# Maxout, output and w1·w_out products of a pooled-attention kernel: pairs of float16 scaled by powers of two in place of pairs of float32r

## The chip, the cores and the metric

The kernel runs on one core of one Trainium2 chip. Its time is the device time of one launch, in microseconds, as the median of three runs. The engines in the profile are PE (TensorE: matmuls, with PEld for the loads of stationary operands), DVE (VectorE), ACT (ScalarE), POOL (GpSimd) and SP (SyncE, which issues the DMAs). "hi" and "lo" below are the two halves of a number that is split so that two short numbers together carry its digits.

## The reference

```python
# attention: B=4, N=384*32=12288 queries, C=128, kv pooled 4x4 -> 768 keys a batch
kv_pool = kv.reshape(B, H // r, r, W // r, r, C).mean(axis=(2, 4))
k = v = kv_pool.reshape(B, -1, C) @ w_sr
s = (q @ k.transpose(0, 2, 1)) / sqrt(C)
a = exp(s - s.max(-1)); a /= a.sum(-1) + 1e-9
x = (a @ v).reshape(B * N, C)                       # 49152 x 128
# maxout: w1, w2, w3 are 128 x 768, w_out is 768 x 128
h = maximum(maximum(x @ w1, x @ w2), x @ w3)
out = h @ w_out
```

The four maxout weights arrive as float64; the kernel reads their 64-bit words as integers and builds float32 from them itself.

## The kernel before

**Tiles.** The 49152 queries go through in 96 groups of 512 (`NG`), 24 to a batch. A group is turned so that channels lie on the partitions. For each group there are four score tiles of 128 queries by 768 keys (six matmuls of 384 columns each, into `ps_s`), a softmax, the product with the values (`attend`, 18 matmuls of 512 columns into `ps_x`), and the maxout part in six slices `f` of 128 hidden units.

**Maxout.** With d2 = w2 − w1 and d3 = w3 − w1 the hidden value is x·w1 + max(0, x·d2, x·d3). So `hidden` (L610) makes two products a slice, x·d2 and x·d3, `hidden_first` (L621, ACT) and `hidden_max` (L626, DVE) take max(0, ·, ·), `hidden_hi` (L631, ACT) and `hidden_lo` (L636, POOL) split the result, and `project` (L691) multiplies by w_out. The part x·w1·w_out comes from one 128×128 matrix `w1o`, made once by `product_w1` (L259), and is added after the last slice.

**Pairs.** Scores and values already use pairs of float16. The maxout products use pairs of float32r: x as `xh`, `xl` (L594, L602), the d's as `d_hi`, `d_lo`, h as `hh`, `hl`, w_out as `wo`, and `w1o`. Every product is three matmuls: hi·hi, hi·lo, lo·hi. That gives 36 + 18 + 3 = 57 float32r matmuls of 512 columns a group.

**Order.** Nothing is reordered by a scheduler: every engine runs its instructions in the order of the program (`InOrder`, L94). The table `ORDER` (L151) writes out, for twelve slices (two groups), which step is issued when: H hidden, R relu, M max, C hi, L lo, O project, S scores, m/e/c/l softmax, X attend, xh/xl the split of x, P/G/T the output, q. the queries, k the keys of the next batch. `WEIGHTS` (L149) is such a table for the start: for each of the four weights and both halves, at which point n the steps of taking the 64-bit words apart are issued (power_bits, power_float, sign, join, rest). The points 0 to 22 lie in the written-out start (L792 to L879), the later ones in the first slices through `late` (L881).

**Buffers.** `ps_h` has two banks, one for each of the two products of a slice, so the next slice's first product needs the relu of this one, and its second needs the max. `spare(True)` (L112) borrows one of these banks for small matmuls. `ps_s` has two double banks, `ps_x` and `ps_o` one bank each.

**Keys.** For each batch a class `Keys` pools kv, finds one power of two from the largest pooled value (`size`, `sized`), and splits the projected keys. For batches 1 to 3 its steps are spread over the groups r of the batch before by `keys_step` (L1004).

Of the kernel before, what the change touches and what calls it, by code (L numbers as in the profile page):

```python
# [9 lines left out]
F32 = mybir.dt.float32  # L10
F32R = mybir.dt.float32r
# [10 lines left out]
def kernel(  # L22
# [28 lines left out]

    nc = tc.nc
# [20 lines left out]
    X_UP, O_DOWN = 2.0 ** -24, 2.0 ** -10  # L73
# [41 lines left out]
    def pow2(t, src):  # L115

        dve.tensor_scalar(
            out=t.bitcast(I32), in0=src.bitcast(I32), scalar1=EXPO, scalar2=None, op0=ALU.bitwise_and
        )
        dve.tensor_scalar(out=t, in0=t, scalar1=TINY, scalar2=HUGE, op0=ALU.max, op1=ALU.min)  # L120
# [11 lines left out]
    x_up = const.tile([C, 1], F32, name="x_up")  # L132
    d_hi = [[const.tile([C, HALF_F], F32R, name=f"d{i}{h}_hi") for h in range(2)] for i in (2, 3)]
    d_lo = [[const.tile([C, HALF_F], F32R, name=f"d{i}{h}_lo") for h in range(2)] for i in (2, 3)]
    w1T = [const.tile([P, HALF_F], F32, name=f"w1T{h}") for h in range(2)]
    w1o = const.tile([C, 2, C], F32R, name="w1o")
    e_bias = const.tile([P, 1], F32, name="e_bias")
    wo = [const.tile([P, NFT // 2, 2, C], F32R, name=f"wo{h}") for h in range(2)]
# [5 lines left out]
    JOIN_ON_POOL, REST_ON_DVE, LO_ON_DVE, HI_ON_DVE, HL_ON_DVE, W_HI_ON_DVE = ((0, 2, 6), (0,), (3,), (6, 8), (), ())  # L144
# [4 lines left out]
    WEIGHTS = {(0, 0): (10, 12, 15, 18, 20), (1, 0): (19, 20, 20, 20, 21), (2, 0): (21, 21, 21, 21, 22), (0, 1): (19, 21, 22, 23, 23), (1, 1): (22, 23, 24, 24, 24), (2, 1): (25, 25, 25, 25, 25), (3, 0): (25, 25, 26, 26, 26), (3, 1): (26, 26, 27, 27, 27)}  # L149
# [17 lines left out]
    def sr_weights():  # L167
        e = prep.tile([C, C], F32, name="sr_e")
        dve.tensor_scalar(
            out=e.bitcast(I32), in0=wsr_sb.bitcast(I32), scalar1=EXPO, scalar2=None, op0=ALU.bitwise_and  # L170
# [8 lines left out]
        times(x_up, ps[:, :1], X_UP)  # L179
# [17 lines left out]
    class Weights64:  # L197
# [40 lines left out]

        def rest(self):
            if self.hi is None:  # L240
                return
            if not self.wide:
                dve.tensor_tensor(
                    out=self.r1.bitcast(F32), in0=self.r1.bitcast(F32), in1=W[0, self.h].r1.bitcast(F32),
                    op=ALU.subtract,
                )
            on = dve if self.n in REST_ON_DVE else pool
            r1 = self.lay(self.r1.bitcast(F32))
            copy_on("dve" if self.n in W_HI_ON_DVE else "act")(out=self.hi, in_=r1)
            on.tensor_tensor(out=self.lo, in0=r1, in1=self.hi.bitcast(F32), op=ALU.subtract)  # L250

    def turn_w1(h):

        ps = spare(True)
        for t in range(NFT // 2):
            tr(out=ps[:, t * P:(t + 1) * P], in_=W[0, h].r1.bitcast(F32)[:, t * P:(t + 1) * P], identity=ident)
        act.copy(out=w1T[h], in_=ps[:, :HALF_F])

    def product_w1():  # L259
# [13 lines left out]
    class Keys:  # L273


        def __init__(self, b):
# [6 lines left out]
            self.g = tiny.tile([P, 1], F32, name="g", bufs=2)  # L283
            self.up = tiny.tile([P, 1], F32, name="k_up", bufs=2)
# [47 lines left out]
        def gathered_size(self):  # L332
            ps = spare(True)
            for s in range(KS):
                mm(out=ps[:, :1], lhsT=ones, rhs=self.m[:, s:s + 1], start=s == 0, stop=s == KS - 1)
            self.sized(ps[:, :1])
# [42 lines left out]
        def size(self):  # L379
            ps = self.spare()  # L380
            for s in range(KS):
                mm(out=ps[:, :1], lhsT=ones, rhs=self.m[:, s:s + 1], start=s == 0, stop=s == KS - 1)

        def sized(self, ps):
# [4 lines left out]
                out=self.g, in0=self.g, scalar1=TINY, scalar2=2.0 ** -12, op0=ALU.max, op1=ALU.mult  # L389
# [204 lines left out]
    def attended_hi(g):  # L594
        ps = st["x"][g]
        assert g == 0 or st["parts"] == 1
        xh = xp.tile([C, G], F32R, name="xh")
        act.mul(out=xh, in_=ps, mul=x_up)
# [22 lines left out]
    def hidden_first():  # L621
        h1 = hp.tile([P, G], F32, name="h1", bufs=2)
        act.activation(out=h1, in_=st["hp"].pop(0), func=AF.Relu)
        return h1

    def hidden_max(h1):  # L626
        h = hp.tile([P, G], F32, name="h", bufs=4)
        dve.tensor_tensor(out=h, in0=st["hp"].pop(1), in1=h1, op=ALU.max)
        return h

    def hidden_hi(g, f):  # L631
        hh = hp.tile([P, G], F32R, name="hh", bufs=HB_)
# [3 lines left out]
    def hidden_lo(g, f):  # L636
        h, hh = st["h"][g, f]
        hl = hp.tile([P, G], F32R, name="hl", bufs=HB_)
        (dve if g * NFT + f in HL_ON_DVE else pool).tensor_tensor(out=hl, in0=h, in1=hh.bitcast(F32), op=ALU.subtract)
        st["h"][g, f] = (hh, hl)  # L640

    def last_hidden():
# [13 lines left out]
        for half in range(2):  # L656
            h1 = hp.tile([P, G], F32, name="h1", bufs=2)[:, :n]
            act.activation(out=h1, in_=ps[half][0], func=AF.Relu)
            h.append(hp.tile([P, G], F32, name="h", bufs=4)[:, :n])
            dve.tensor_tensor(out=h[half], in0=ps[half][1], in1=h1, op=ALU.max)  # L660
        for half in range(2):
            hh.append(hp.tile([P, G], F32R, name="hh", bufs=HB_)[:, :n])
            act.copy(out=hh[half], in_=h[half])
            hl.append(hp.tile([P, G], F32R, name="hl", bufs=HB_)[:, :n])
# [101 lines left out]
    W = {}  # L766
# [326 lines left out]
```

## Time and profile before

| | |
|---|---|
| runs | 2123.61, 2122.72, 2119.67 us; median 2122.72 us |
| the profiled execution | 2117.23 us, of which its span 2115.5 us |
| instructions in the span | 29124 |
| ACT, POOL busy | 1485.8 us (70%), 1502.0 us (71%) |
| first attend of 512 columns on PE | 93.49 us after the span's start |
| DMA | 283.29 MB in 839959 packets, mean 134 GB/s |

The slices of the span show three stages: a start of some 100 us, in which the keys of the first batch, the queries and the weights are prepared and PE is busy about six tenths of the time; a long even stretch of groups; and an end of some 12 us. In the profile's rows a matmul's duration includes the filling and emptying of the array, so it overlaps its neighbours; how fast PE takes matmuls is read from the distance of their starts. Nearly every instruction is recorded through the helper at L102, so groups are told apart by their tiles, not by lines.

### The profile page before, as it was taken

What the parts mean: (1) busy time and instruction counts of PE and PEld (TensorE: products, weight loads), DVE (VectorE), ACT (ScalarE), POOL (GpSimd) and SP (SyncE); (2) the same over time, 40 slices, a digit from 0 to 9 for tenths busy, and PEclk for the clock granted to TensorE, in tenths of its full rate; (3) what the DMA queues carried; (4) which work ended last, traced back from release to release, by engine and by line L of the source; (5) the groups of instructions that cost most, each with busy time, mean ns of one, the idle gap of its engine ahead of it and who ended that gap; (6) DMA issues with size and microseconds to landing.
All of it is one profiled execution on the core that took longest, in us unless ns stands there. A gap on an engine that the chain in (4) does not pass through costs nothing.

```text
span 2115.5 us, 29124 instructions
## 1 busy us (share of the span) xinstructions
PE 2070.2 (98%) x9797; PEld 1407.4 (67%) x9797; DVE 1536.5 (73%) x2438; ACT 1485.8 (70%) x2535; POOL 1502.0 (71%) x1070
## 2 busy tenths in 40 slices
PE   6699999999999999999999999999999999999998
PEld 5366666666666666666666666666666666666666
DVE  5678877776777887777776887777777776777675
ACT  2477777777777777777777777777777777777774
POOL 2577777777777777777777777777777777777764
PEclk8899999999999999999999999999999999999999
DMA  8278655555567755655656775555555555565652
GB/s 257 49 166 179 155 126 119 135 123 130 117 140 184 167 126 129 131 121 119 134 126 155 166 172 124 117 130 129 130 119 121 131 129 123 118 134 124 127 111 63
DMA packets 839959, 283.29 MB, mean 134 GB/s; under 512 B 813441, under 2 KB 814593, under 8 KB 839809
## 3 DMA queue, kind: packets, MB, share of 16 engines
q1 hardware_dynamic: 839808, 281.43, 59.4%
q8 instruction: 77, 1.26, 0.2%
q14 instruction: 74, 0.60, 0.1%
HBM read 53.54 MB, written 25.17 MB: 37 GB/s over the span
## 4 chain that ended last, share of the span: by engine, by line
PE 94%; DVE 2%; DMA 1%; ACT 1%; POOL 1%; issue 0%; SPq 0%; DVEq 0%; ACTq 0%; POOLq 0%
PE ps_h L102 37%; PE ps_o L102 21%; PE ps_x L102 18%; PE ps_s L102 17%; DMA aT<-ahl 1%; DVE kv_piece L102 1%; POOL ahl L102 1%; ACT ahl L102 0%; DMA kv_piece<-in_kv_dram 0%; ACT a L102 0%; DVE o_sb L102 0%; DVE w_e L102 0%; DVE mx L102 0%; DVE q_row L102 0%; POOL q_sb L102 0%
## 5 line engine op out<-in xcount | busy, mean ns | idle before, releaser
L102 POOL TENSOR_TENSOR hl<-h,hh 128x512 fp32r<-128x512 f32 x575 | 751.5, 1318 | 217.9 <-ACT hh L102 216.8
L102 POOL TENSOR_TENSOR ahl<-a,ahl 128x768 f16<-128x768 f32 x383 | 631.9, 1661 | 309.1 <-issue 182.5
L102 ACT ACTIVATE h<-ps_h 128x512 f32<-128x512 f32 x575 | 342.4, 596 | 285.9 <-PE ps_h L102 284.3
L102 PE MATMUL ps_h<-xh,d_hi 128*128 128x512 f32 x1150 | 523.2, 455 | 5.9 <-ACT w1T L102 3.2
L102 DVE TENSOR_TENSOR h<-ps_h,h 128x512 f32<-128x512 f32 x575 | 396.9, 690 | 181.1 <-PE ps_h L102 112.4
L102 ACT CAST hh<-h 128x512 fp32r<-128x512 f32 x577 | 350.5, 616 | 170.0 <-DVE h L102 170.0
L102 DVE TENSOR_REDUCE mx<-ps_s 128x1 f32<-128x768 f32 x383 | 364.7, 952 | 130.7 <-PE ps_s L102 130.5
L102 PE MATMUL ps_h<-xh,d_lo 128*128 128x512 f32 x1150 | 455.2, 396 | 0.4 <-POOL d_lo L102 0.4
L102 PE MATMUL ps_h<-xl,d_hi 128*128 128x512 f32 x1150 | 453.6, 394 | 0.8 <-DVE xl L102 0.8
L102 ACT ACTIVATE a<-ps_s,nb,q_sc 128x768 f32<-128x768 f32 x383 | 378.2, 990 | 45.3 <-DVE nb L102 43.7
L102 PE MATMUL ps_x<-aT,v_hi 128*128 128x512 f16 (+1 forms) x1188 | 379.3, 377 | 14.0 <-DMA aT<-ahl 13.9
L102 PE MATMUL ps_s<-k_hi,qT 128*128 128x384 f16 x1532 | 379.2, 330 | 7.3 <-ACT a L102 6.4
L102 PE MATMUL ps_o<-hh,wo 128*128 128x512 f32 x1140 | 374.1, 409 | 0.1
L102 PEld LDWEIGHTS <-qT 128*128 128x128 f16 x2304 | 195.9, 98 | 209.6 <-issue 110.5
L102 ACT CAST ahl<-a 128x768 f16<-128x768 f32 x382 | 312.2, 831 | 5.6 <-DMA aT<-ahl 1.2
L102 PEld LDWEIGHTS ps_h<-xh,d_hi 128*128 128x128 f32 x1150 | 217.6, 189 | 74.2 <-ACT w1T L102 3.6
L102 PEld LDWEIGHTS ps_h<-xl,d_hi 128*128 128x128 f32 x1150 | 216.1, 188 | 54.7 <-DVE xl L102 1.3
L102 PE MATMUL ps_s<-k_lo,qT 128*128 128x384 f16 x766 | 250.5, 327 | 0.3 <-DVE k_lo L102 0.3
L102 PEld LDWEIGHTS ps_o<-hh,wo 128*128 128x128 f32 x1140 | 212.0, 188 | 51.6 <-POOL wo L102 0.6
L102 PEld LDWEIGHTS ps_h<-xh,d_lo 128*128 128x128 f32 x1150 | 217.4, 189 | 36.1 <-POOL d_lo L102 0.9
L102 PEld LDWEIGHTS <-v_hi 128*128 128x128 f16 x1188 | 116.5, 99 | 172.7 <-issue 58.7
L102 PE MATMUL ps_o<-hl,wo 128*128 128x512 f32 x570 | 223.1, 391 | 0.0
(129 smaller groups left out, 1843.8 us busy)
## 6 DMA issues: line engine op xcount, KB each, us to landing
kv_piece<-in_kv_dram SPq DMA_DIRECT2D x48, 512.0 KB, 4.6
q_sb<-in_q_dram SPq DMA_DIRECT2D x48, 512.0 KB, 4.1
out_dram<-o_sb SPq DMA_DIRECT2D x95, 256.0 KB, 2.1
aT<-ahl SPq DMA_TRANSPOSE x384, 3.4
kv_piece<-in_moe_w_dram SPq DMA_DIRECT2D x6, 384.0 KB, 5.7
qT<-q_hl SPq DMA_TRANSPOSE x96, 3.2
o_turned<-o_planes SPq DMA_TRANSPOSE x95, 3.1
kv_piece<-in_moe_w_out_dram SPq DMA_DIRECT2D x2, 384.0 KB, 4.0
```

The source lines that it names most:

```text
L102: return lambda **kw: tc.keep_in_program_order(op(**kw))
```

## The change

The tiles `xh`, `xl`, `d_hi`, `d_lo`, `hh`, `hl`, `wo` and `w1o` become float16. Float16 has a short range of exponents, so the numbers are scaled by powers of two that are taken from the data at the start: one for each half of the d's (`size_d`, from the largest d of the half, each row weighed by the column factor `col` of w_sr), and one for w_out (`size_u`). The fixed factors `X_UP` and `H_DOWN` keep x and h in range, and the output is scaled back by `w_down`. What was an ACT cast and a POOL subtraction for the six weight splits becomes an ACT multiplication and a DVE `scalar_tensor_tensor`.

```diff
-    X_UP, O_DOWN = 2.0 ** -24, 2.0 ** -10
+    X_UP, H_DOWN, O_DOWN = 2.0 ** -20, 2.0 ** -14, 2.0 ** -10
+    D_TOP, U_TOP, SMALL, LARGE = 2.0 ** 14, 2.0 ** 11, 2.0 ** -60, 2.0 ** 60
...
-    d_hi = [[const.tile([C, HALF_F], F32R, name=f"d{i}{h}_hi") for h in range(2)] for i in (2, 3)]
+    d_hi = [[const.tile([C, HALF_F], F16, name=f"d{i}{h}_hi") for h in range(2)] for i in (2, 3)]
...
-    WEIGHTS = {(0, 0): (10, 12, 15, 18, 20), (1, 0): (19, 20, 20, 20, 21), (2, 0): (21, 21, 21, 21, 22), ...
+    WEIGHTS = {(0, 0): (10, 12, 15, 18, 20, 21), (1, 0): (19, 20, 20, 20, 21, 21, 22), (2, 0): (21, 21, 21, 21, 21, 22, 22), ...
+    SIZE = {22: 0, 25: 1, 27: 2}
...
         def rest(self):
...
-            copy_on("dve" if self.n in W_HI_ON_DVE else "act")(out=self.hi, in_=r1)
-            on.tensor_tensor(out=self.lo, in0=r1, in1=self.hi.bitcast(F32), op=ALU.subtract)
+            if self.n % 4 in (1, 2):
+                dve.tensor_tensor(out=self.values(), in0=self.values(), in1=W[0, self.h].values(), op=ALU.subtract)
+        def top(self):
+            t = u_top[:, self.h:self.h + 1] if self.wide else d_top[:, self.h, self.n % 4:self.n % 4 + 1]
+            dve.tensor_reduce(out=t, in_=self.values(), axis=AX.X, op=ALU.max, apply_absolute_value=True)
+        def split(self):
+            v, up = self.lay(self.values()), (u_up if self.wide else d_up)[self.h]
+            act.mul(out=self.hi, in_=v, mul=up)
+            dve.scalar_tensor_tensor(out=self.lo, in0=v, scalar=up, in1=self.hi, op0=ALU.mult, op1=ALU.subtract)
+    def size_d(h):
+        top = d_top[:, h]
+        dve.tensor_reduce(out=top[:, 3:4], in_=top[:, :3], axis=AX.X, op=ALU.max)
+        times(top[:, 3:4], top[:, 3:4], col)
+        ps = spare(True)
+        mm(out=ps[:, :1], lhsT=ones, rhs=top[:, 3:4], start=True, stop=True)
+        pow2(d_size[h], ps[:, :1], SMALL, LARGE)
+        dve.reciprocal(out=d_up[h], in_=d_size[h])
+        times(d_up[h], d_up[h], col, D_TOP)
+    def size_u():
+        ratio = tiny.tile([P, 1], F32, name="ratio")
+        dve.reciprocal(out=ratio, in_=d_size[0])
+        times(ratio, ratio, d_size[1])
+        times(u_top[:, 1:2], u_top[:, 1:2], ratio)
+        ps = spare(True)
+        for h in range(2):
+            mm(out=ps[:, :1], lhsT=ones, rhs=u_top[:, h:h + 1], start=h == 0, stop=h == 1)
+        size = tiny.tile([P, 1], F32, name="u_size")
+        pow2(size, ps[:, :1], SMALL, LARGE)
+        times(w_down, size, d_size[0], 2.0 ** 10 / (D_TOP * U_TOP))
+        dve.reciprocal(out=u_up[0], in_=size)
+        times(u_up[0], u_up[0], U_TOP)
+        times(u_up[1], u_up[0], ratio)
+        times(w1o_up, d_up[0], u_up[0], H_DOWN)
...
-            self.sized(ps[:, :1])
+            self.turn_tops(True)
+            self.tops()
+            self.size(True)
+            self.sized()
...
-        act.mul(out=xh, in_=ps, mul=x_up)
+        act.mul(out=xh, in_=ps, mul=X_UP)
...
-        act.activation(out=h1, in_=st["hp"].pop(0), func=AF.Relu)
+        act.activation(out=h1, in_=st["hp"].pop(0), func=AF.Relu, scale=H_DOWN)
...
-        dve.tensor_tensor(out=h, in0=st["hp"].pop(1), in1=h1, op=ALU.max)
+        dve.scalar_tensor_tensor(
+            out=h, in0=st["hp"].pop(1), scalar=H_DOWN, in1=h1, op0=ALU.mult, op1=ALU.max
+        )
...
-        hl = hp.tile([P, G], F32R, name="hl", bufs=HB_)
+        hl = hp.tile([P, G], F16, name="hl", bufs=HB_)
...
-        dve.tensor_tensor(out=o, in0=o, in1=rs.unsqueeze(2).to_broadcast([P, NJ, C]), op=ALU.mult)
+        dve.scalar_tensor_tensor(
+            out=o, in0=o, scalar=w_down, in1=rs.unsqueeze(2).to_broadcast([P, NJ, C]), op0=ALU.mult, op1=ALU.mult
+        )
```

The keys' largest value is now found by turning a column of row maxima with a matmul, one reduction, and a matmul that spreads it (`turn_tops`, `tops`, `size`), in place of three summing matmuls. In `keys_step` the steps from `peak` to `values` move: peak from r = 10 to 9, the size over r = 10 to 12, `project` from 11 and 12 to 12 and 13, `values` from 13 to 14. On SP that moves the two transposes of the keys one group later, past the other transposes of that group; nothing else moves there.

Three places in the order of the engines matter. The first is a slice of the even stretch on PE: the end of one `hidden` and one `project`. A float32r matmul carries its weight load in itself; before:

```order
L102 MATMUL ps_h<-xh,d_hi 128x512
L102 MATMUL ps_h<-xh,d_lo 128x512
L102 MATMUL ps_h<-xl,d_hi 128x512
L102 MATMUL ps_o<-hh,wo_121 128x512 x2
L102 MATMUL ps_o<-hl,wo_121 128x512
```

The same slice now, in which each float16 matmul has its weight load as an instruction ahead of it:

```order
L103 LDWEIGHTS d_hi
L103 MATMUL ps_h<-xh,d_hi 128x512
L103 LDWEIGHTS d_lo
L103 MATMUL ps_h<-xh,d_lo 128x512
L103 LDWEIGHTS d_hi
L103 MATMUL ps_h<-xl,d_hi 128x512
L103 LDWEIGHTS wo_130
L103 MATMUL ps_o<-hh,wo_130 128x512
L103 LDWEIGHTS wo_130
L103 MATMUL ps_o<-hh,wo_130 128x512
L103 LDWEIGHTS wo_130
L103 MATMUL ps_o<-hl,wo_130 128x512
```

The matmuls are the same and stand in the same order. The second place is on DVE in the start, from the split of the first group's x (`xl`) to the first max (`h`); `kv_piece` holds the weights' words and `w_e` their exponents. Before:

```order
L102 SCALAR_TENSOR_TENSOR xl<-ps_x,x_up,xh 128x512
L102 TENSOR_TENSOR kv_piece<-kv_piece 128x384
L102 SCALAR_TENSOR_TENSOR w_e<-kv_piece,w_e 128x384
L102 TENSOR_SCALAR kv_piece<-kv_piece 128x384
L102 TENSOR_SCALAR w_e<-kv_piece 128x384
L102 TENSOR_TENSOR h<-ps_h,h_508 128x512
```

Now, from the same last step on `w_e` on:

```order
L103 TENSOR_SCALAR w_e<-kv_piece 128x384
L103 TENSOR_REDUCE d_top<-d_top 128x1
L103 TENSOR_SCALAR d_top<-d_top,col 128x1
L103 TENSOR_SCALAR d_size<-ps_h 128x1
L103 TENSOR_SCALAR d_size<-d_size 128x1
L103 RECIPROCAL d_up<-d_size 128x1
L103 TENSOR_SCALAR d_up<-d_up,col 128x1
L103 SCALAR_TENSOR_TENSOR d_lo<-kv_piece,d_up,d_hi 128x384 x2
L103 SCALAR_TENSOR_TENSOR h<-ps_h,h_532 128x512
```

Between the weights' words and the first max now stand the search for the size, with a matmul of PE in its middle (`d_size<-ps_h`), and both lo splits. The third place is on PE at the first `project`, after the `hidden` of the slice f = 4 of the first group. Before:

```order
L102 MATMUL ps_h<-xh,d_lo 128x512
L102 MATMUL ps_h<-xl,d_hi 128x512
L102 MATMUL ps_o<-hh,wo_120 128x512 x2
L102 MATMUL ps_o<-hl,wo_120 128x512
L102 MATMUL ps_o<-hh,wo_120 128x512 x2
```

Now:

```order
L103 MATMUL ps_h<-xl,d_hi 128x512
L103 MATMUL ps_h<-u_top,ones 128x1 x2
L103 LDWEIGHTS wo_130
L103 MATMUL ps_o<-hh,wo_130 128x512
L103 LDWEIGHTS wo_130
L103 MATMUL ps_o<-hh,wo_130 128x512
```

The two matmuls on `u_top` need the largest value of both halves of w_out, so the projections behind them, and the first attend behind those, now stand behind the second half's words too.

More of the change, by code (lines that the diff above doesn't have):

```diff
@@ L119, in pow2 @@
         )
-        dve.tensor_scalar(out=t, in0=t, scalar1=TINY, scalar2=HUGE, op0=ALU.max, op1=ALU.min)
+        dve.tensor_scalar(out=t, in0=t, scalar1=low, scalar2=high, op0=ALU.max, op1=ALU.min)
     def times(t, src, by, by2=None):
@@ L178, in sr_weights @@
         mm(out=ps[:, :1], lhsT=col_row[:1], rhs=ones[:1, :1], start=True, stop=True)
-        times(x_up, ps[:, :1], X_UP)
+        times(col, ps[:, :1], 1.0)
     def load64(w, h, wide):
@@ L237, in join, with values @@
                 dve.tensor_tensor(out=self.r1, in0=self.r1, in1=self.e, op=ALU.bitwise_or)
+        def values(self):
+            return self.r1.bitcast(F32)
         def rest(self):
[L240 to L247, printed above, removed]
@@ L377, in peak, with turn_tops, tops, size @@
             )
[L379 to L384, printed above, removed]
+        def turn_tops(self, first=False):
+            self.tops_ps = spare(first)
+            dve.tensor_reduce(out=self.m[:, KS:KS + 1], in_=self.m[:, :KS], axis=AX.X, op=ALU.max)
+            mm(out=self.tops_ps[:1, :P], lhsT=self.m[:, KS:KS + 1], rhs=ident, start=True, stop=True)
+        def tops(self):
+            dve.tensor_reduce(out=self.top, in_=self.tops_ps[:1, :P], axis=AX.X, op=ALU.max)
+        def size(self, first=False):
+            self.size_ps = spare(first)
+            mm(out=self.size_ps[:, :1], lhsT=ones[:1], rhs=self.top, start=True, stop=True)
+        def sized(self):
+            ps = self.size_ps[:, :1]
             dve.tensor_scalar(
@@ L388, in sized @@
             dve.tensor_scalar(
-                out=self.g, in0=self.g, scalar1=TINY, scalar2=2.0 ** -12, op0=ALU.max, op1=ALU.mult
+                out=self.g, in0=self.g, scalar1=TINY, scalar2=2.0 ** -13, op0=ALU.max, op1=ALU.mult
             )
@@ L596, in attended_hi @@
         assert g == 0 or st["parts"] == 1
[L597 to L598 removed]
+        xh = xp.tile([C, G], F16, name="xh")
+        act.mul(out=xh, in_=ps, mul=X_UP)
         st["xh"][g] = xh
@@ L603, in attended_lo @@
         ps, xh = st["x"][g], st["xh"].pop(g)
-        xl = xp.tile([C, G], F32R, name="xl")
+        xl = xp.tile([C, G], F16, name="xl")
         dve.scalar_tensor_tensor(
-            out=xl, in0=ps, scalar=x_up, in1=xh.bitcast(F32), op0=ALU.mult, op1=ALU.subtract
+            out=xl, in0=ps, scalar=X_UP, in1=xh, op0=ALU.mult, op1=ALU.subtract
         )
@@ L755, in last_finish @@
             dve.tensor_tensor(out=osb[:, half], in0=o[:, :, 0], in1=lo, op=ALU.add)
-            dve.tensor_tensor(
-                out=osb[:, half], in0=osb[:, half], in1=rs[:, half].unsqueeze(2).to_broadcast([P, n, C]), op=ALU.mult
+            dve.scalar_tensor_tensor(
+                out=osb[:, half], in0=osb[:, half], scalar=w_down,
+                in1=rs[:, half].unsqueeze(2).to_broadcast([P, n, C]), op0=ALU.mult, op1=ALU.mult,
             )
@@ L769, in weights @@
         for (i, h), at in WEIGHTS.items():
-            for step, m in enumerate(at):
+            for step, m in enumerate(at[:6]):
                 if m == n:
                     w = W[i, h]
-                    (w.power_bits, w.power_float, w.sign, w.join, w.rest)[step]()
+                    (w.power_bits, w.power_float, w.sign, w.join, w.rest, w.top)[step]()
+        if n in SIZE:
+            size_u() if SIZE[n] == 2 else size_d(SIZE[n])
+        for (i, h), at in WEIGHTS.items():
+            if len(at) > 6 and at[6] == n:
+                W[i, h].split()
     def load_w(h, which=range(3)):
@@ L1020, in keys_step @@
                 n.add(s, 2 * step, 2 * step + 1, us=us)
-        if r == 10 and f in (0, 2, 3):
+        if r == 9 and f in (0, 2, 3):
             n.peak(max(f - 1, 0))
-        before = {7: (n.turn, 0), 9: (n.turn, 1), 11: (n.project, 0), 12: (n.project, 1)}
-        after = {7: (n.turned, 0), 9: (n.turned, 1), 11: (n.projected, 0), 12: (n.projected, 1)}
+        before = {7: (n.turn, 0), 9: (n.turn, 1), 12: (n.project, 0), 13: (n.project, 1)}
+        after = {7: (n.turned, 0), 9: (n.turned, 1), 12: (n.projected, 0), 13: (n.projected, 1)}
         if f == 5:
```

65 lines of the change are left out of this document (38 added, 27 removed).

## The prediction

> **What bounds the kernel now.** I read the page first, then the waits and windows of the long stretch, then the timeline of one group. The page's busy times, and the waits of PE between 130 and 2080 us:
>
> ```profile
> PE 2070.2 (98%) x9797; PEld 1407.4 (67%) x9797; DVE 1536.5 (73%) x2438; ACT 1485.8 (70%) x2535; POOL 1502.0 (71%) x1070
> PE ps_x L102 <- DMA aT<-ahl: 1.0, 2, 0.5
> 950.00:1150.00 200.00, 200.00 (x942) 135.13 (x941) 142.83 (x225) 144.31 (x246) 146.19 (x104) 1.00 0.61 135
> ```
>
> PE waits 1.0 us in 1950. The third row is a window: PE busy in 200.00 of 200 us, then PEld, DVE 142.83, ACT 144.31, POOL 146.19, and the granted clock 1.00. So in the long stretch PE alone sets the pace, and its pace is the distance of matmul starts. From PE's timeline, float32r first (the first and the last of six matmuls), then float16 of the same 512 columns (the first and the last of eight), then float16 of 384 columns (the first and the last of four; a row with x2 lies between):
>
> ```profile
> 1000.82 0.39 PE L102 MATMUL ps_h<-xh,d_lo 128*128 128x512 f32 x1
> ...
> 1001.98 0.39 PE L102 MATMUL ps_o<-hh,wo 128*128 128x512 f32 x1
> ...
> 1003.60 0.38 PE L102 MATMUL ps_x<-aT,v_lo 128*128 128x512 f16 x1
> ...
> 1005.11 0.38 PE L102 MATMUL ps_x<-aT,v_hi 128*128 128x512 f16 x1
> ...
> 1031.20 0.33 PE L102 MATMUL ps_s<-k_lo,qT 128*128 128x384 f16 x1
> ...
> 1031.69 0.33 PE L102 MATMUL ps_s<-k_lo,qT 128*128 128x384 f16 x1
> ```
>
> Five steps take 1.16 us, so 0.232 us for a float32r matmul. Seven take 1.51, so 0.2157 for a float16 one, whose weights also change at every matmul. Three take 0.49, so 0.163 for a score matmul. One group is read from the chain that ended last, where the same nine attend matmuls come two groups apart:
>
> ```profile
> 1003.53 1.96 PE ps_x L102 x9
> ...
> 1045.68 1.96 PE ps_x L102 x9
> ```
>
> 42.15 us for two groups, 21.08 for one. The sum agrees: 57 × 0.232 + 18 × 0.2157 + 24 × 0.163 = 13.22 + 3.88 + 3.91 = 21.01; the missing 0.07 lies at the changes between the two types.
>
> **The change part by part.** *The matmuls.* All 57 become float16 with a weight load of their own, which is what the attend matmuls are. So a group takes 75 × 0.2157 + 24 × 0.163 = 16.18 + 3.91 = 20.09 us, 0.99 less. Groups 1 to 95 run at PE's pace: 95 × 0.99 = 94 us. About 1 us of this is lost before 133 us, where an attend still waits for its DMA. **−93 us.** Bounds: without the 0.07 of type changes the saving is 95 × 57 × 0.0163 = 88; and the 1.51 us may be 0.005 less by its last digit, 0.0007 a matmul, 75 × 0.0007 × 95 = 5, so 99 at the most.
>
> A rule of the Trainium skill stands against the size of this. The page "TensorE: Matmul & The Clock Gate", section "Back-to-back issue gap", gives N/2.4 + 2.5 ns for a single matmul, 216 ns at N = 512, which the float16 rows match, and beside it about 131 ns at N = 512 for a sustained stream of weight loads and matmuls. By the second figure, an estimate, the 75 matmuls would take 9.8 us a group in place of 16.18. The sustained float16 stream of this trace shows 0.2157.
>
> *Does anything else become the bound?* DVE per group is 142.83 / 200 × 21.08 = 15.1 us. The max becomes a `scalar_tensor_tensor`. These rows price it:
>
> ```profile
> L102 DVE TENSOR_TENSOR h<-ps_h,h 128x512 f32<-128x512 f32 x575 | 396.9, 690 | 181.1 <-PE ps_h L102 112.4
> L102 DVE SCALAR_TENSOR_TENSOR xl<-ps_x,x_up,xh 128x512 fp32r<-128x512 f32 x96 | 72.1, 751 | 172.6 <-ACT xh L102 172.6
> 48.38 0.56 DVE L102 SCALAR_TENSOR_TENSOR kv_piece<-kv_piece 128x384 int32<-128x384 int32 x1
> 48.97 0.56 DVE L102 TENSOR_TENSOR kv_piece<-kv_piece,w_e 128x384 int32<-128x384 int32 x1
> L102 POOL TENSOR_TENSOR hl<-h,hh 128x512 fp32r<-128x512 f32 x575 | 751.5, 1318 | 217.9 <-ACT hh L102 216.8
> L102 POOL TENSOR_TENSOR ahl<-a,ahl 128x768 f16<-128x768 f32 x383 | 631.9, 1661 | 309.1 <-issue 182.5
> ```
>
> With a fixed factor the two forms cost the same (0.56); with a factor read from a tile, as in `xl`, 751 against 690. So between 0 and +61 ns a max, at most 0.4 us a group, and as much again for `o_sb`: DVE stays under 15.6 of 20.09. I take it as hidden under PE; without that cover it would cost 575 × 0.061 = 35 us over the run. POOL's `hl` now reads and writes float16: `ahl`, which does so, takes 2.16 ns an element against 2.57, so POOL gets lighter, by at most 0.2 us an operation. ACT keeps its counts; `xh` loses the factor read from a tile. All of it lies beside PE.
>
> *The handoffs.* Two banks of `ps_h` go back and forth each slice. The relu and the max of one slice, and the matmuls that reuse their banks:
>
> ```profile
> 1030.36 0.60 ACT L102 ACTIVATE h<-ps_h 128x512 f32<-128x512 f32 x1 [0.92 <-PE ps_h L102]
> 1031.16 0.69 DVE L102 TENSOR_TENSOR h<-ps_h,h 128x512 f32<-128x512 f32 x1 [0.29 <-PE ps_h L102]
> ...
> 1032.55 0.39 PE L102 MATMUL ps_h<-xh,d_hi 128*128 128x512 f32 x1
> ...
> 1033.25 0.40 PE L102 MATMUL ps_h<-xh,d_hi 128*128 128x512 f32 x1
> ```
>
> The relu ends at 1030.96 and its bank is written at 1032.55: 1.59 us to spare. The max ends at 1031.85, its bank is written at 1033.25: 1.40. A slice of nine matmuls gets 0.15 us shorter and the max up to 0.06 longer, so 1.2 us stay. I cost this at nothing. The softmax chain must keep up too, with 1 us a group less; PE's two waits for `aT`, 1.0 us in all, say that it is ahead nearly everywhere.
>
> *The keys of later batches.* Two small DVE operations more a batch, at 154 ns (below), and a small matmul less; the transposes on SP come one group later, ten groups ahead of their use at r = 24. Nothing.
>
> *The start.* Here PE waits for the others, and the change adds to them. The rows: the first half's subtraction, the first max, PE's first project and first 512-column attend, and prices.
>
> ```profile
> 49.63 0.56 DVE L102 TENSOR_TENSOR kv_piece<-kv_piece 128x384 f32<-128x384 f32 x1
> 58.13 0.69 DVE L102 TENSOR_TENSOR h<-ps_h,h 128x512 f32<-128x512 f32 x1 [1.16 <-PE ps_h L102]
> 84.77 0.73 PE L102 MATMUL ps_o<-hh,wo 128*128 128x512 f32 x2
> 90.99 0.56 DVE L102 TENSOR_TENSOR kv_piece<-kv_piece,w_e 128x384 int32<-128x384 int32 x1
> 93.49 0.59 PE L102 MATMUL ps_x<-aT,v_hi 128*128 128x512 f16 x1 [6.41 <-DMA aT<-ahl]
> L102 DVE TENSOR_REDUCE mx<-ps_h 128x1 f32<-128x384 f32 x2 | 1.0, 547 | 0.0
> L102 DVE TENSOR_SCALAR g<-g 128x1 f32<-128x1 f32 x4 | 0.6, 154 | 0.1
> L102 PE MATMUL ps_h<-pool_max,ones 128*128 128x1 f32 x6 | 0.9, 240 | 0.1
> sum 40.00, PE 23.35 PEld 13.90 DVE 24.49 ACT 19.15 POOL 19.58; mean PE 5.84 PEld 3.48 DVE 6.12 ACT 4.79 POOL 4.90
> 87.24 1.42 DVE L102 SCALAR_TENSOR_TENSOR w_e<-kv_piece,w_e 128x384 int32<-128x384 int32 x1
> ```
>
> DVE gets 8 reductions (0.55), 6 lo splits (0.56 to 0.6, were POOL's) and 24 small operations (0.17 with the gap): 4.4 + 3.5 + 4.1 = 12 us. PE gets small matmuls in the middle of these chains, about 0.4 us each with both ways. Followed along the order: the key size costs +0.8 us (two small operations and a matmul more). The first max waited for one cast and one POOL subtraction; now three reductions (1.7), a DVE that stands at POOL's join ahead of `xl` (1.5), the size with its matmul (1.5) and two casts and two lo splits (1.7) come before it: near 65 in place of 58.13, **+7**. The second half adds three reductions, a size and two splits, with the `turn_w1` transposes and the next scores queued behind its matmul on PE: +3. Then the last row of w_out's words, 90.99, comes near 101, and behind it a reduction, ten small operations, a matmul and a split (0.55 + 2.3 + 1.1): projects begin near 104 and take 2.5 us, and the attend that started at 93.49 starts near 106: **+12.5 us**. It no longer waits for `aT`, which lands near 105 by the same shift.
> Bounds: +2, if DVE's idle time takes it up (the sum row is the window 60 to 100: DVE busy 24.49 of 40, 15.5 us idle, more than the 12 added); +20, if all of it is serial with 8 us of new waits. I take 12.5, because the order puts each chain ahead of something that PE needs.
>
> The last row is a DVE operation of 0.55 us that took 1.42 while POOL worked on `ahl`. The Trainium skill, "GPSIMD Engine Reference", section "1. Specifications", says that POOL shares its SBUF interfaces with VectorE and contends with VectorE instructions that have two SBUF inputs. The six moved splits are such instructions; by the rule up to 6 × 0.87 = 5 us more, and the row agrees. The bound of +20 stands without it.
>
> *The end.* The last group's chain keeps its form; its matmuls of 256 columns gain some 0.5 us, which I leave out.
>
> Sum, against the profiled execution's own time: 2117.2 − 93 + 12.5 = 2036.7 us. The median of the runs is 2122.7, 5.5 above it; nothing in the change touches that difference, so I add it whole: 2122.7 − 80.5 = **2042 us**.
>
> **The rivals.** *A handoff becomes the bound* (9%). Near the end of the run slices come without scores and the spare times are smallest; a DVE or ACT that is late there, or in the groups that also prepare keys, makes PE wait. For: DVE would be at 78%. Against: 1.2 us to spare per slice. If half of the 570 slices lost their gain of 0.16, 46 us go back: 2088.
>
> *The change does not do what it says, and the time ends on the other side* (3%). If the 0.232 comes not from the type but from where these matmuls stand (a new bank every three, weights from constant tiles, waits on semaphores), the float16 ones keep it. Then only the start's +12.5 is left: 2135. The point from which it decides: a gain per matmul under 12.5 / 5415 = 2.3 ns makes the kernel slower. Against: the attend matmuls change weights as often, the scores change banks every three, and both run at the float16 pace.
>
> *Float16 next to float16 goes faster than any row here* (1%). The stream then stops binding and DVE's 15.5 us a group does: 2122.7 + 12.5 − 95 × 5.6 = 1603. The page of the Trainium skill named above has such a figure, 131 ns; no run here shows it.
>
> **How the numbers follow.** Forecast 86%: 2042, with its own range from 2027 (the start at +2, the matmuls at −98 with the lost 1 us) to 2056 (the start at +20, the matmuls at −87). The rivals hold 13%, the last per cent is no change. The range of 8 in 10 is this, a little wider towards the first rival: 2026 to 2058. A measurement here tells 0.2% (4 us) from no change. Faster is the forecast, the first rival and the last, less 1% for a handoff that takes all: 95%; within 0.2% 1%; slower 4%, the second rival and that.
>
> **What would show it.** In the profile after: starts of `ps_h` matmuls 0.2157 apart; the same nine `ps_x` matmuls 40.2 us apart over two groups; PE's waits from 145 us on still a few us in all; the first 512-column attend near 106 us, with PE waiting there for `u_top` or `wo` in place of `aT`; DVE's max between 690 and 751 ns; POOL's `hl` below 1318. I am wrong if the starts stay at 0.232, if `ps_h` shows waits for the DVE or ACT `h` in the long stretch, or if the granted clock there falls below 1.00: at 20.09 / 21.08 = 0.95 of it the gain would be gone.

## The result and the profile after

| | before | after |
|---|---|---|
| median of four runs | 2121.19 us | 2059.85 us (2057.64 to 2062.03) |
| ratio, 95% interval | | 0.971, 0.9693 to 0.9727 |
| profiled execution | 2117.23 us | 2062.03 us |

The kernel got faster by 61 us in place of 80. The page of the changed kernel, busy times first, then the groups that answer to the prediction's prices:

```profile
PE 1981.9 (96%) x9797; PEld 967.2 (47%) x9797; DVE 1510.4 (73%) x2482; ACT 1457.4 (71%) x2535; POOL 1409.2 (68%) x1064
...
L103 POOL TENSOR_TENSOR hl<-h,hh 128x512 f16<-128x512 f32 x575 | 670.1, 1176 | 205.1 <-ACT hh L103 204.8
L103 DVE SCALAR_TENSOR_TENSOR h<-ps_h,h 128x512 f32<-128x512 f32 x575 | 396.5, 690 | 186.4 <-ACT h L103 90.5
...
L103 PE MATMUL ps_h<-xh,d_hi 128*128 128x512 f16 x1150 | 437.7, 381 | 7.6 <-ACT w1T L103 5.9
```

PE's share fell from 98 to 96%: it waits more than before. The max is at the low end of its bounds (690 ns), POOL's `hl` got lighter (1176 ns), and of the 7.6 us that `ps_h` matmuls waited in the whole run 5.9 are one wait in the start. PE's pace, from its timeline (the first and the last of six products into `ps_h` and `ps_x`):

```profile
999.67 0.38 PE L103 MATMUL ps_h<-xh,d_lo 128*128 128x512 f16 x1
...
1000.75 0.38 PE L103 MATMUL ps_x<-aT,v_hi 128*128 128x512 f16 x1
```

Five steps take 1.08 us, 0.216 each, and there is no extra step where `ps_h` gives way to `ps_x`. What PE waited for between 130 and 2030 us, and three windows (PE busy first, granted clock third from the end, share of the DMA engines next):

```profile
PE ps_x L103 <- DMA aT<-ahl: 13.7, 16, 2.3
PE ps_x L103 <- DVE pool_max L103: 3.4, 3, 1.1
PE ps_x L103 <- issue: 1.3, 2, 0.7
PE ps_s L103 <- ACT a L103: 0.4, 1, 0.4
```

```profile
350.00:550.00 200.00, 199.67 (x983) 96.39 (x982) 144.52 (x240) 147.66 (x257) 143.90 (x109) 1.00 0.67 132
950.00:1150.00 200.00, 199.16 (x981) 95.73 (x980) 144.98 (x232) 148.19 (x258) 145.07 (x110) 1.00 0.70 140
1130.00:1230.00 100.00, 96.53 (x473) 45.75 (x471) 80.04 (x126) 72.01 (x126) 72.99 (x54) 1.00 0.81 174
```

Where kv is loaded for the next batch (1130 to 1230), PE loses 3.5 us in 100; elsewhere hardly any.

A ledger from PE's timeline: when the first matmul of the attend of groups 1, 4 and 94 starts, and what lies between.

| stretch | before | after | difference | of it pace |
|---|---|---|---|---|
| start to attend 1 | 93.49 | 112.80 | +19.31 | 0 |
| attend 1 to 4 | 60.76 | 58.95 | −1.81 | 3 × −0.985 |
| attend 4 to 94 | 1905.78 | 1835.10 | −70.68 | 90 × −0.985 |
| attend 94 to the span's end | 55.42 | 53.40 | −2.02 | all |
| span | 2115.45 | 2060.25 | −55.20 | |

A group in which nothing waits takes 20.09 us, in place of 21.07. Over the 90 groups the time beyond 90 such periods, the excess below, was 9.2 us before (8.0 of it in the groups that do the keys' small matmuls) and is 27.2 now. So pace gives −93.6, the start +19.3, and new waits behind it +19.1 (18.0 in the 90 groups, 1.1 ahead of them).

### The profile page after: what moved, and what is told of

It reads as the page before. It is cut to its first block, busy times and chain, and to the rows that moved or that the text cites. A ratio compares the mean times of both kernels' runs of the same rounds, so it can differ in the third digit from the quotient of the medians.

```text
span 2060.3 us, 29166 instructions
## 1 busy us (share of the span) xinstructions
PE 1981.9 (96%) x9797; PEld 967.2 (47%) x9797; DVE 1510.4 (73%) x2482; ACT 1457.4 (71%) x2535; POOL 1409.2 (68%) x1064
## 4 chain that ended last, share of the span: by engine, by line
PE 78%; DVE 8%; ACT 5%; DMA 5%; issue 2%; POOL 2%; SPq 0%; DVEq 0%; ACTq 0%; POOLq 0%
PE ps_h L103 30%; PE ps_o L103 17%; PE ps_x L103 16%; PE ps_s L103 15%; DMA aT<-ahl 4%; DVE h L103 1%; ACT ahl L103 1%; DVE kv_piece L103 1%; DVE q_row L103 1%; ACT a L103 1%; POOL ahl L103 1%; DVE mx L103 1%; ACT hh L103 1%; ACT xh L103 1%; ACT h L103 1%
## 5 line engine op out<-in xcount | busy, mean ns | idle before, releaser
L103 POOL TENSOR_TENSOR hl<-h,hh 128x512 f16<-128x512 f32 x575 | 670.1, 1176 | 205.1 <-ACT hh L103 204.8
L103 DVE SCALAR_TENSOR_TENSOR h<-ps_h,h 128x512 f32<-128x512 f32 x575 | 396.5, 690 | 186.4 <-ACT h L103 90.5
L103 ACT CAST hh<-h 128x512 f16<-128x512 f32 x577 | 349.8, 615 | 167.6 <-DVE h L103 167.4
L103 DVE TENSOR_REDUCE mx<-ps_s 128x1 f32<-128x768 f32 x383 | 365.4, 954 | 112.4 <-PE ps_s L103 111.9
L103 PE MATMUL ps_h<-xh,d_hi 128*128 128x512 f16 x1150 | 437.7, 381 | 7.6 <-ACT w1T L103 5.9
L103 PE MATMUL ps_h<-xh,d_lo 128*128 128x512 f16 x1150 | 437.7, 381 | 0.0
L103 PE MATMUL ps_h<-xl,d_hi 128*128 128x512 f16 x1150 | 437.6, 380 | 0.0
L103 PEld LDWEIGHTS <-d_hi 128*128 128x128 f16 x2308 | 226.2, 98 | 258.8 <-issue 2.8
L103 PE MATMUL ps_o<-hh,wo 128*128 128x512 f16 x1140 | 340.5, 381 | 2.3 <-DVE wo L103 2.3
L103 PE MATMUL ps_x<-aT,v_lo 128*128 128x512 f16 (+1 forms) x594 | 222.7, 376 | 0.0
L103 PE MATMUL ps_o<-hl,wo 128*128 128x512 f16 x570 | 216.9, 380 | 0.0
L103 PEld LDWEIGHTS <-v_hi 128*128 128x128 f16 x1188 | 116.8, 99 | 149.7 <-DMA aT<-ahl 9.6
```

The lines of the kernel that those rows point to most:

```text
L103: return lambda **kw: tc.keep_in_program_order(op(**kw))
```

## The experiments on the long stretch

My theory: the waits for `aT` (the transposed softmax, brought by DMA) come from 512 KB loads of queries and of kv (keys and values) that are under way just ahead of the last `aT` transpose of a group. The rivals: the softmax chain itself is late, or the moved key steps are. SP's queue around the attend of group 53, which waited 1.82 us; first after, then the same group before (start, then how long the issue took):

```profile
1165.98 0.91 SPq L103 DMA_DIRECT2D kv_piece<-in_kv_dram  x1
1166.99 1.27 SPq L103 DMA_TRANSPOSE qT<-q_hl  x1
1168.31 0.58 SPq L103 DMA_DIRECT2D q_sb<-in_q_dram  x1
1169.10 3.07 SPq L103 DMA_TRANSPOSE aT<-ahl  x1
```

```profile
1184.07 0.59 SPq L102 DMA_DIRECT2D kv_piece<-in_kv_dram  x1
1184.76 1.26 SPq L102 DMA_TRANSPOSE qT<-q_hl  x1
1186.07 0.57 SPq L102 DMA_DIRECT2D q_sb<-in_q_dram  x1
1187.75 1.49 SPq L102 DMA_TRANSPOSE aT<-ahl  x1
```

The order is the same. Before, the transpose came 1.68 us behind the query load and took 1.49 us to issue; now it comes 0.79 us behind and takes 3.07. And the chain of the wait, after: softmax halves on ACT and POOL, then a DMA of 6.46 us (the median of `aT` is 4.0), then the attend.

```profile
1167.47 1.60 POOL ahl L103
1169.08 0.03 POOL hl L103
1169.10 6.46 DMA aT<-ahl
1175.56 0.05 issue
1175.61 1.47 PE ps_x L103 x6
```

**The query load earlier.** `qd` goes from the end of the last slice of the odd group to the end of its slice f = 2; its buffer is free there.

```diff
-        "H l P L k C R T e M m O S X c",
+        "H l P L k C R T e M m O S X c qd",
...
-        "H xh m C L xl l c e R M O S X k qd",
+        "H xh m C L xl l c e R M O S X k",
```

> The changed kernel with one thing moved: the load of the next queries is issued at the end of the odd group's slice f=2 in place of its slice f=5, where it stands just ahead of the last transpose of the softmax (aT) in SP's queue. My theory: the loss in the long stretch (PE's waits for aT, 13.7 us in 16 times between 130 and 2030 us) comes from 512 KB loads that stand in front of the aT transposes, and the faster PE has 0.4 us less room for them. Then these waits fall to 2 to 7 us and the time falls by 7 to 12 us, to near 2050. Rival 1, the softmax chain itself (max, exp, both halves) is late: waits and time stay within 2 us. Rival 2, the loads of kv alone do it: the time falls by under 3 us.

Measured: span 2051.2, 9.1 us less; the waits of PE in the same stretch:

```profile
PE ps_x L103 <- DMA aT<-ahl: 4.3, 4, 2.4
PE ps_x L103 <- DVE pool_max L103: 3.4, 3, 1.1
PE ps_s L103 <- DMA qT<-q_hl: 1.3, 2, 0.7
```

The waits for `aT` fell into the expected 2 to 7 us, and the excess over the 90 groups from 27.2 to 17.0. Ahead of them the move costs: attend 1 to 4 takes 61.05 us in place of 58.95. PE waits 2.40 us for `aT` there, in one piece, in place of 1.11 and 0.72, and from 139.00 to 142.20, behind the wait, its granted clock is 0.50. The median is 2054.41 us, ratio 0.9691 (0.9677 to 0.9706), 5.4 us under that of the change where 7 to 12 were expected; the traced execution of the change was its slowest, so the 9.1 lies on the high side. The intervals touch, so the times alone would not settle it; the waits do.

**The same edit in the kernel before.**

> The kernel before with only the query load moved to the end of the odd group's slice f=2. The theory that PE's pace exposes the load: at 21.07 us a group the transposes have 0.4 us more room, only 1.3 us of waits stood in the stretch, so it gains at most 1.5 us there, and the time is the same within 0.2%. If the load costs about 10 us whatever the pace: near 2110.

Measured: 2118.53 us, ratio 0.9996 (0.9986 to 1.0005), excess 8.4 against 9.2 (here too attend 1 to 4 got longer, 62.26 us against 60.76). In the 90 groups of the traces the same load in the same place cost 0.8 us in the kernel before and 10.2 in the changed one. So the place of the load alone is not what went wrong; the change made it matter. That it is the pace, and no other part of the change, is argued.

**The query load on another queue.**

```diff
-        sp_dma.dma_start(out=t, in_=q_src[s])
+        (act if s > 2 else sp_dma).dma_start(out=t, in_=q_src[s])
```

> The changed kernel with the query loads (from the fourth on) issued by ACT at the same place of the program, so that they go by another queue and no longer stand ahead of the aT transposes in SP's. It tells order in the queue from use of the DMA engines. If the order in SP's queue makes aT late: the waits for aT fall as with the earlier load (13.7 to about 4 us), time about 5 us less. If the transfers compete for the DMA engines themselves: the waits stay above 10 us and the time is the same or longer, with about 48 issues on ACT more.

Measured: 2059.45 us, ratio 0.9719 (0.9703 to 0.9736), the same time as the change and so nearer to the second: waits for `aT` 10.0 us, excess 22.9. ACT reaches the load earlier than SP did, so the run doesn't part queue from engines cleanly. The same group 53, in SP's queue:

```profile
1165.11 0.87 SPq L103 DMA_DIRECT2D kv_piece<-in_kv_dram  x1
1166.10 1.25 SPq L103 DMA_TRANSPOSE qT<-q_hl  x1
1168.23 3.06 SPq L103 DMA_TRANSPOSE aT<-ahl  x1
```

The query load went out on ACT's queue at 1165.18, 3.05 us ahead of the transpose, and the issue still took 3.06 us; but here a kv load stands in SP's own queue as well, 3.12 us ahead. The 36 odd groups (of 4 to 94) with a query load and no kv load ahead of the last transpose tell more, in medians over the traces: the issue took 2.22 us after and 1.45 here, where 1.43 is the time without any load, and from issue to landing it was 4.60 us after and 4.08 here, where 3.67 is the time without any load. So from the other queue, and 0.8 us further ahead, the load hardly stretches the issue any more, but the landing still comes later: a place in another queue is not enough, the transfers compete as well. How much of the rest is queue and how much distance stays open; the kernel before, with the load 2.35 us ahead in SP's own queue, shows 1.56 (1.40 without any load). The Trainium skill, "DMA: Bandwidth & Descriptors", section "Issuing engines are not separate DMA queues", says that DMAs of all issuing engines run on the same 16 DMA engines and interleave; the 4.08 us against 3.67 agree.

**The kv loads.** In the groups r = 1 to 6 the second kv load goes from slice f = 4 to f = 2.

```diff
-        if f in (1, 4) and 1 <= r <= 6:
-            m = 2 * (r - 1) + f // 4
+        if f in (1, 2) and 1 <= r <= 6:
+            m = 2 * (r - 1) + f // 2
```

> The changed kernel with the second kv load of a group issued in slice f=2 in place of f=4 (the groups r=1 to 6 of batches 0 to 2). My theory (loads in front of the aT transposes, the query load and the kv loads together): most of the waits stand in the groups with kv loads, so the waits for aT fall from 13.7 to 4 to 9 us and the time by 5 to 9 us. If only the query load counts: under 3 us. If the softmax chain is late by itself: no change.

Measured: a miss, 2067.04 us, ratio 0.9749 (0.9734 to 0.9763), 7 us longer than the change. The waits for `aT` fell as expected, to 5.2 us, but the load now stands ahead of the queries' transposes:

```profile
PE ps_s L103 <- DMA qT<-q_hl: 7.9, 6, 2.6
PE ps_x L103 <- DMA aT<-ahl: 5.2, 8, 2.5
```

The wait moved to another transpose, and the attends of groups 3 and 4 came 2.4 us later. The trace is of the fastest of the four executions, its span only 1.4 us over that of the change; what the others lost beyond that it does not show.

**Both loads, and the key maxima.** The reduction of the key maxima to one column (the first step of `turn_tops`) goes from slice f = 5 of r = 10, where PE's next matmul waits for it, to f = 4 of r = 9.

```diff
+        def top_row(self):
+            dve.tensor_reduce(out=self.m[:, KS:KS + 1], in_=self.m[:, :KS], axis=AX.X, op=ALU.max)
...
         def turn_tops(self, first=False):
...
-            dve.tensor_reduce(out=self.m[:, KS:KS + 1], in_=self.m[:, :KS], axis=AX.X, op=ALU.max)
...
+        if r == 9 and f == 4:
+            n.top_row()
```

> The changed kernel with the moves of both loads, and with the reduction of the key maxima to one column a group earlier than the matmul that turns it. Theory: the waits for aT fall under 3 us, the three waits for pool_max (3.4 us in all) go, and the time falls by 13 to 17 us, to near 2045. If the chain of the softmax is late by itself: only the 3.4 us go.

> The kernel before with the moves of both loads. Its PE waits for aT only 1.0 us in the long stretch (1.85 us with the smallest gaps counted), so the theory that the pace of PE exposes the loads gives at most 2 us less, 2119 to 2121, the same. If the loads cost time in themselves, whatever the pace, it is faster by more than 5 us.

Measured: 2065.64 us, ratio 0.9747 (0.9731 to 0.9763), and for the kernel before 2128.7, ratio 1.0042 (1.0027 to 1.0057), 0.4% slower. Both expectations missed. With both loads moved the `qT` waits are 10.5 us in the changed kernel (2.8 in the kernel before), and the first groups lose time: attend 4 comes at 176.98 in place of 171.75 in the changed kernel, at 162.3 in place of 154.3 in the kernel before, where PE's waits for `aT` between the first attend and attend 4 are 5.93 us in place of 0.52. In the 90 groups the `aT` waits of the changed kernel are down to 0.6 us, so the loads make nearly all of them. The waits for `pool_max` did go.

**The query load and the key maxima**, with the kv loads in their place:

> The changed kernel with the query load at the end of the odd group's slice f=2 (as in the run with that alone, span 2051.2 us) and the reduction of the key maxima to one column a group ahead of its matmul; the kv loads stay. The three waits for pool_max (3.4 us) go and nothing comes in their place: span near 2048, time 3 us below the run with the query load alone. Rival: the matmul or the next attend then waits for something else, and the time is the same within 1 us.

Measured: 2049.57 us, ratio 0.9664 (0.9651 to 0.9677), span 2047.8. The interval lies wholly below that of the change, so this version beats both kernels. Its waits:

```profile
PE ps_x L103 <- DMA aT<-ahl: 3.6, 3, 2.2
PE ps_s L103 <- DMA qT<-q_hl: 1.2, 3, 0.6
PE ps_x L103 <- issue: 1.1, 1, 1.1
PE ps_s L103 <- ACT a L103: 0.4, 1, 0.4
```

Excess 12.8 us in the 90 groups, against 9.2 before: of 18.0 new us in the stretch two small moves take back 14.4. Ahead of it 1.9 us are lost again: attend 1 to 4 takes 60.83 us in place of 58.95. As with the query load alone there is one wait of 2.19 us for `aT`, and a granted clock of 0.50 behind it (139.80 to 143.10).

## The experiments on the start

DVE's share up to the first attend, in windows that end there; before, after, with constant scales, and with constant scales and no lo splits (the window, its length, then PE, PEld, DVE, ACT, POOL, granted clock):

```profile
46.00:93.49 47.49, 26.39 (x133) 17.41 (x132) 34.52 (x61) 20.81 (x39) 23.32 (x19) 0.82 0.26 59
```

```profile
46.00:112.80 66.80, 31.32 (x152) 16.93 (x151) 49.43 (x99) 23.96 (x44) 20.54 (x16) 0.66 0.24 48
```

```profile
46.00:102.65 56.65, 28.66 (x151) 14.52 (x149) 41.38 (x69) 24.16 (x44) 20.41 (x16) 0.77 0.28 57
```

```profile
46.00:98.59 52.59, 29.23 (x144) 15.17 (x143) 37.43 (x62) 22.37 (x41) 19.72 (x15) 0.69 0.30 60
```

DVE's busy time grew by 14.9 us and its idle time by 4.4 (13.0 to 17.4): together the 19.3.

**Constant scales.** The core of the edit:

```diff
-    SIZE = {22: 0, 25: 1, 27: 2}
+    SIZE = {}
...
-                    (w.power_bits, w.power_float, w.sign, w.join, w.rest, w.top)[step]()
+                    (w.power_bits, w.power_float, w.sign, w.join, w.rest, lambda: None)[step]()
```

> The changed kernel without the search for the sizes of the weights: the eight reductions, the two sizes of the d's and the size of w_out are left out, and the scales are constants (128 and 16, the values that these inputs give); the splits with the new scales stay. It prices the search in the start, where the first 512-column attend came at 112.80 us against 93.49 before. Theory: the search stands serially in DVE's and PE's chains; three reductions and a size for each half (about 3.65 us each) and one reduction and a size for w_out (about 3.8 us) go, so the first attend comes near 102 and the time falls by 9 to 13 us. Rival: DVE's idle time hides most of the search and the moved splits and the order are what costs: the first attend stays above 108.

> The run with constant scales, and the six lo splits of the weights (d_lo and the second halves of wo) left out as well, set to zero at the start on POOL. It prices the splits that moved from POOL to DVE: six by 0.57 to 0.63 us are 3.6 us of DVE. If they stand in the chain one for one the first attend comes near 99 (102.65 with them); if DVE's idle time takes them, it stays above 101.5. What is then left over 93.49 is neither search nor lo splits.

Measured: first attend 102.65 with constant scales, 98.59 without the lo splits as well. So of the 19.3 us the search is 10.15 and the moved splits are 4.06, both in series as the theory said; 5.1 are neither. The whole gained less than its start, and less than the 9 to 13 us expected: 2055.09 us (ratio 0.9696, 0.9681 to 0.9710), 4.8 us in the medians, the traced span 8.6 us shorter. Without the lo splits a single run gave 2052.96, its span only 0.5 us below that with constant scales: attend 4 starts at 161.93 against 162.65. So 3.3 of the 4.06 us are lost again between these two attends. It is not the waits for `aT` that grew there (2.35 us against 2.57) but the time at a lower granted clock, third from the end in these windows of the run without lo splits:

```profile
98.59:140.14 41.55, 38.59 (x183) 18.38 (x184) 25.70 (x43) 28.34 (x52) 24.75 (x19) 0.95 0.73 142
140.40:143.80 3.40, 3.40 (x10) 1.16 (x9) 1.19 (x1) 0.06 (x1) 2.20 (x2) 0.50 0.98 278
```

With constant scales alone the clock is 1.00 from 102.65 to 142.34 and behind that. A clock of 0.95 over 41.55 us and of 0.50 over 3.40 are 2.1 and 1.7 us of PE's time (an estimate: the length times what is missing to 1.00).

**Words later.** The second half's first steps on w1 and w2 go behind the first max.

```diff
-(0, 1): (22, 22, 22, 23, 23, 23), (1, 1): (22, 23, 24, 24, 24, 24, 25)
+(0, 1): (23, 23, 23, 23, 23, 23), (1, 1): (23, 23, 24, 24, 24, 24, 25)
```

> The changed kernel with the first steps on the second half's w1 (exponent, sign, and the exponent of its w2) behind the first max in place of ahead of the splits of the first half. It tells order from amount of work in the start. The first max then comes about 2 us earlier (67.2 to 65.2). If DVE's amount of work sets the first attend, that stays at 112 to 113.5 and the time is the same; if the lateness of the first max is passed on, the first attend comes near 111 and the time falls by 2 us.

Measured: first max 65.12 in place of 67.19, first attend 112.83 in place of 112.80, ratio 0.9719 (0.9706 to 0.9733), the same as the change. The 2 us at the first max do not reach the first attend: the steps that were moved still stand on DVE ahead of w_out's size.

**Joins on POOL**, on top of the two moves of the last run of the part above (the query load and the key maxima). A join puts a weight's sign, exponent and digits together; its last step is what moves.

```diff
-    JOIN_ON_POOL, LO_ON_DVE, HI_ON_DVE, HL_ON_DVE = ((0, 2, 6), (3,), (6, 8), ())
+    JOIN_ON_POOL, LO_ON_DVE, HI_ON_DVE, HL_ON_DVE = ((0, 2, 3, 5, 6, 7), (3,), (6, 8), ())
```

> The same with three more of the weights' joins (w2 and w_out's first half, and both of the second half's that were on DVE before it) given from DVE to POOL. If DVE's work binds the start (49.4 of the 66.8 us up to the first attend), 1.7 us less of it brings the first attend 1 to 2 us forward. If the chain of dependencies binds it, each join on POOL costs 0.4 us more and a handoff, and the first attend comes 1 to 3 us later. I expect the second by a little; in either case under 3 us in the time.

Measured: first attend 116.63 in place of 112.80, median 2054.31, ratio 0.9682 (0.9669 to 0.9695). (The three joins are those of both halves of w_out and of the second half of w2.) Less work on DVE, and later by 3.8 us, more than either expectation, and the median is 4.7 us over that of the run it builds on, where under 3 were expected. At the three joins DVE now idles 1.18, 1.18 and 1.19 us for POOL, in place of working 0.56, 0.56 and 1.39: that is 1.0 of the 3.8 us. Another 0.6 stand at the first max already, ahead of all three; the rest is not traced. What the run shows is that less work on DVE does not bring the first attend forward.

**The attend ahead of the projects.** In slice 4 of group 0 PE gets the size of w_out first, then the attend, then the projects.

```diff
-            if g < 2:
+            if g < 2 and n != 4:
                 late(n)
...
+                if (g, f, token) == (0, 4, "O"):
+                    late(4)
+                    step("X", g, f)
+                if (g, f, token) != (0, 4, "X"):
+                    step(token, g, f)
```

> The changed kernel with the first 512-column attend issued on PE between the two matmuls of w_out's size and the first projects, in place of behind the projects. Theory: PE waits there for wo (to 109.3 us) while aT has landed by about 108, so the first attend starts near 108, the projects follow near 112, and everything behind moves up by about 2.4 us. Rival: aT itself is late there, the attend starts after 111 and the time is the same or up to 2 us longer.

Measured: the attend starts at 108.20, as expected, but the 2.4 us do not come: 2059.42, ratio 0.9712 (0.9698 to 0.9727), the same as the change. The chains, after, and with the edit:

```profile
109.33 3.63 PE ps_o L103 x9
112.96 3.88 PE ps_x L103 x18
116.84 1.29 PE ps_h L103 x6
```

```profile
108.20 6.64 PE ps_x L103 x18
114.85 1.94 PE ps_o L103 x9
116.79 1.29 PE ps_h L103 x6
```

Both reach the next `hidden` at 116.8. PE had just waited some 6 us in both (6.37 us for `u_top` after, 6.17 with the edit), and what comes first after that runs slowly: the attend's 18 matmuls take 6.64 us in place of 3.88. PE's windows there, with the edit and after (granted clock third from the end):

```profile
108.00:113.00 5.00, 4.79 (x12) 1.79 (x13) 2.63 (x9) 4.22 (x8) 0.05 (x1) 0.50 0.00 0
113.00:118.00 5.00, 5.00 (x24) 2.19 (x23) 1.31 (x3) 1.12 (x3) 2.41 (x2) 0.95 0.27 56
```

```profile
108.00:113.00 5.00, 3.67 (x10) 1.39 (x11) 2.22 (x5) 4.21 (x8) 0.71 (x1) 0.56 0.00 0
113.00:118.00 5.00, 5.00 (x25) 2.28 (x24) 0.49 (x1) 1.07 (x2) 0.50 (x1) 1.00 0.25 56
```

The clock is 0.50 there, for the whole window with the edit and for most of it after. The Trainium skill, "TensorE: Matmul & The Clock Gate", section "Part 1: The HAM clock gate", has PE at half its clock after idling until it has been busy for about 3.4 us. The half agrees; the length does so only roughly: by the clocks of these windows the full clock is back at about 112.4 us after and 113.5 with the edit, 3.1 and 5.3 us behind the first of these matmuls. So the earlier start moved the slow stretch forward and made it longer, and nothing was won.

## Why the prediction was right or wrong

*The matmuls: right.* −93 was forecast, pace gave −93.6. The rate of the neighbours of the same type held to the last digit, the 0.07 us of type changes went as well, and the granted clock stayed at 1.00. The rival in which float16 next to float16 runs faster did not come true, nor the one in which the matmuls keep the pace of float32r.

*"I cost this at nothing" (relu and max): right.* No `ps_h` matmul shows up among PE's waits of the long stretch. The rival that a handoff becomes the bound fell for these; in the groups that prepare keys a late DVE did make PE wait, by the 3.4 us below.

*"The softmax chain must keep up too … it is ahead nearly everywhere": the step that failed most.* It was costed at nothing and cost 18.0 us with the keys' part below. Two waits of 1.0 us in all told that the chain was on time, not how much it had to spare. I worked out that room for `ps_h` (1.2 us a slice) and not for the attend. The traces have it. In the 38 of the groups 4 to 94 that have no load in the 8 us ahead of the last `aT` transpose, this landed 1.71 us (median) ahead of the attend before, and 0.78 after. In one of them, group 48, PE came from the last row maximum (`mx`) to the attend in 13.47 us before and in 12.76 after, while the chain from there to the landed `aT` took 11.75 and 11.98: PE's part shrank, the chain did not. The landing itself even took 3.68 us in place of 3.19 in these groups, for a reason that no run isolates. The loads took the rest: with a query load ahead the room is 0.64 us (2.22 before), and with a kv load beside it 0.07 (0.22 before). The query load, moved alone, gave back 10.2 us of the excess; with the kv loads moved too the waits for `aT` in the 90 groups were down to 0.6 us, but waits of 10.5 us for `qT` came up.

*"The keys of later batches … Nothing": wrong by 3.4 us.* The maxima's reduction on DVE stands directly ahead of a matmul of PE, 1.1 us each time; moved a group forward, the waits were gone.

*The start: +12.5 forecast, +19.3 measured, inside its bound of +20.* First max near 65: 67.19. The row of w_out's words that started at 90.99 before was to come near 101: it starts at 103.88, the second of these rows of DVE's timeline.

```profile
102.86 0.98 DVE L103 SCALAR_TENSOR_TENSOR kv_piece<-kv_piece 128x384 int32<-128x384 int32 x1
103.88 1.39 DVE L103 TENSOR_TENSOR kv_piece<-kv_piece,w_e 128x384 int32<-128x384 int32 x1
105.30 0.55 DVE L103 TENSOR_REDUCE u_top<-kv_piece 128x1 f32<-128x384 f32 x1
```

Projects near 104: 109.33. Some of that is a slip in adding: by the prediction's own terms 101 + 0.55 + 2.3 + 1.1 is 104.95, and with 2.5 us of projects the attend stands near 107.5, at +14. That PE then waits for `u_top` and `wo` and not for `aT` was right:

```profile
106.48 0.58 PE L103 MATMUL ps_h<-u_top,ones 128*128 128x1 f32 x2 [6.37 <-DVE u_top L103]
109.33 1.03 PE L103 MATMUL ps_o<-hh,wo 128*128 128x512 f16 x2 [2.27 <-DVE wo L103]
```

The operations that were priced at 12 us of DVE take 12.0 there (the search 8.34, the lo splits 3.69), but they cost 14.2 of the 19.3 us: the search costs 10.15, since PE's and ACT's steps stand in the same chain. The other 5.1 us had no term in the sum. By the window without search and lo splits, DVE is busy 2.9 us longer than before in them and idle 2.2 us longer. In DVE's rows from 46 us to the first attend the 23 operations that write `kv_piece` add up to 15.6 us against 12.8 before, and to 14.7 without search and lo splits. The contention with POOL that the prediction priced beside the sum has this direction, though no run isolates it, and the six splits for which it was priced took 0.6 us each, as in the sum. A PE at the lower clock adds 1.1 us (projects 3.63 us against the 2.5 forecast). What causes the 5.1 us stays open.

*The base.* I added 5.5 us because the profiled execution of before lay under its median; that of after lies 2.2 above its own. In the profiled executions the sum missed by 25.3 us (2036.7 forecast, 2062.03): 6.8 in the start and 19.1 in new waits, less 0.6 of pace. In the medians it missed by 17.9; that this is less is luck, from which executions were profiled.

## What to carry to other kernels

When the engine that sets the pace gets faster, every wait that ended in time before has to be priced anew with its spare time, DMAs included: look for the smallest distance from landing to use and for what else the DMA engines move just then. A transfer that is not urgent belongs where no urgent one follows closely; another queue alone did not change the time here. In a start that is a chain of small steps, a data-driven scale costs its whole chain, and an engine that is started earlier from idle may only run its slow stretch earlier.

## What the hardware showed

- A float16 matmul of 512 columns with its own weight load starts 0.216 us after the last one, whatever product it belongs to; the same product in float32r took 0.232.
- A 512 KB load 1.6 us ahead of a transpose in the same queue stretched its issue from 1.43 to 2.22 us and its landing from 3.68 to 4.60 us after the start of the issue (medians of the changed kernel); on another queue and 2.4 us ahead it was 1.45 and 4.08 us.
- After a wait of some 6 us PE took 0.43 us a matmul at a granted clock of 0.50, for another 3.1 us of matmuls in one order and 5.3 us in the other.
